# Thresholded attention and a maxout feed-forward on one core: scores negated into z by the maximum pass, the threshold in an instruction of its own, and a new order of issue

## The chip, the core and the metric

The kernel runs on one core of a Trainium2 chip. Its engines are named as in the profile: PE (TensorE, matmuls; PEld is its weight load), DVE (VectorE), ACT (ScalarE), POOL (GpSimd) and SP (SyncE, which here only issues DMAs). The metric is the device time of one execution in microseconds. For a change of this kernel, about 1% is what a measurement can tell from none.

## What is computed

Attention over 8 batches and 8 heads, 576 positions, head width 64, in fp32. In each row of scores, those more than tau (0.02) below the row's maximum are dropped before the softmax. Then a feed-forward layer takes the maximum of three products elementwise and multiplies it by an output matrix.

```python
scale = 1.0 / np.sqrt(q.shape[-1])
scores = scale * np.matmul(q, k.transpose(0, 1, 3, 2))
thresh = np.max(scores, axis=-1, keepdims=True) - tau
scores = np.where(scores >= thresh, scores, -1000000000.0)
scores = scores - np.max(scores, axis=-1, keepdims=True)
attn = np.exp(scores)
attn = attn / (np.sum(attn, axis=-1, keepdims=True) + 1e-09)
attn_out = np.matmul(attn, v)
# x: attn_out as 4608 rows of 512
h = np.maximum(np.maximum(x @ w1, x @ w2), x @ w3)   # 512 to 768
out = h @ w_out
```

## The kernel before

**Tiling.** Four heads of one batch are a quad; there are 16 quads. A quad has nine chunks, each of 128 rows of queries and keys of all pairs that belong together, and each chunk two halves (r = 0 and 1) of 128 rows by 576 scores. So there are 144 chunks and 288 halves; a half is the unit of the softmax.

**The way of a half.** Each step is a letter in the order (below). S: PE writes the scores of a half into one of four PSUM slots of two banks each (line 280, `scores`). m: DVE takes the row maximum out of PSUM (line 307, `maximum`). e: ACT makes the first pass, reads the same PSUM slot and writes z, an fp32 tile in SBUF for both halves of a chunk (line 318, `exponents`). Then the second pass makes the masked numerators in place in z and sums them (line 326, `numerators`). r: DVE takes the reciprocals of the chunk's two sums. p: POOL multiplies z by them and writes P in bf16, one instruction for each half. t: SP issues a DMA that transposes P into the quad's tile ptq. O: PE multiplies ptq by v.

**Two ways for the two passes.** The string MASKED has a digit for every half. For "1", ACT's first pass is an exponential of score minus maximum, and DVE drops what is below exp(-tau) and sums, in one instruction (letter k). For "0", ACT's first pass is a leaky rectifier of the distance below the threshold, with the slope FLAT = 2**-100 on the kept side, and ACT's second pass is an exponential with scale -1/FLAT that brings the kept ones back to their size and the dropped ones to zero, and sums (letter n). Of the 288 digits 97 are ones.

**Maximum.** For masked halves it is a reduction with the sign turned (`nm` is minus the maximum). For the others it is a pass that subtracts tau, keeps the maximum in an accumulator (`nm` is the maximum minus tau, which the rectifier takes as its bias), and writes a bf16 result that nobody reads (`unused`).

**The rest.** T: PE transposes q or k; ACT (a) and DVE (c) take them out of PSUM, POOL swaps the halves of q (q). F and B: PE's feed-forward pieces, first and second part; h (ACT) and v (DVE) take the hidden pieces out, u (ACT) the output rows, o stores them. x and w take the products out. l loads q, k and v, y casts v, g loads a piece of weights, z casts it on POOL.

**The order.** The string ORDER holds one letter for each step, with a digit for the PSUM slot behind S, T, O and F. The program walks through it and issues one step at a time, and `_Ordered` (line 80) keeps each engine's instructions in that order. Nothing is rearranged: an instruction that waits holds up all that stands behind it on its engine. There are four PSUM slots (SLOTS), four z tiles (ZBUFS), six P tiles (PBUFS). In the kernel before, the first quad's loads, transposes and swaps are issued ahead of the order.

The lines that say what is chained to what in the two passes:

```python
scalar.activation(out=zn, in_=sc, func=AF.Exp, bias=bias)                              # masked, first pass
scalar.activation(out=zn, in_=sc, func=AF.Prelu, bias=bias, scale=-1.0, alpha=FLAT)    # not masked, first pass
vector.scalar_tensor_tensor(out=zn, in0=zn, scalar=thr, in1=zn,
                            op0=OP.is_ge, op1=OP.mult, accum_out=acc)                  # masked, second pass
scalar.activation(out=zn, in_=zn, func=AF.Exp, scale=-1.0 / FLAT, accum_out=acc)       # not masked, second pass
```

Of the kernel before, what the change touches and what calls it, by code (L numbers as in the profile page):

```python
# [23 lines left out]
MASKED = """
101001010001010101001000101000011001001100001100001001000010001000001000
000100111100100100010010100000011000100001110011101000000100000001001001
000100010110111000011000100000001101000011110101010000000011000001000001
011001111000110001000010001100000010010000101010100110001000011100010010
"""


# [5 lines left out]
ORDER = """
lllS0lmyeS1lylS2ymllS3kelmnlS0mleS1rlepmlT2kpnlS3elrmpalS0mtepS2meyT1mntS3cqekqnlT1S0mellyarkT2ynlS1mplermlp
eS3lcepS0tmnS2qmS1eqlrmnpS3lkeptnmS0pemlekytS2emT1nrT3mlpnlrcpelkpT3etS0raS2mpnlS1mqetkapS0emS3gnpmS2eryrtkp
eT1mnS0qlcelmpS1nlS3mpntmpermeptS2kepS0nmlS1yertkperS3mnplO2melprmtepS0wnS1qmetS2pmnS3pelrkztnO0memeplS1rknl  # L40
qT2lewmgpakS3gnpS2tmepxrrmS1epT0tmeS3pnkS2ptnmezrmeS1keqgT3cnS2pamS0npmtS3eprmeS1pmteS2pmeS0myteT3knO1znlrcl
emS3plnrO2lpmngwpekpxS1teS0rwmF2npS3mteqBrmepS1khF0qteF2mnBpS3evqBnmF1pS0nrvztBemS2phS3rgempF1nmF0ptBekzBevS
2nS3rvpnF1gmpF0ntBmzeBekS2pghF3rmnS1ptveBzmF0nS2vpeBgrmT3ptS1hazmT0eS3cqegF2mpT0BkatF1nzvS0eBrrmpnS2gvS3pemO
1qntrmeznF0wpT2geBrcpnS1S3pthmS2npmO0eytmqekpS1eF3wrxmS2qBepmF0nF1yvtpeBS3znvBlnrF2pmlhS0lrpBetmF1pnS3vzeBtm
S2npvS0nlpmF1elmetkS3eS2rnrmplS0BlmpelmpetS3kepF2mnlkutT0eBkarrokpuS3luS0rmouS1pmoO2epmetqeT3pwS0nocT1pS2atm
qO3nmqepT1xwS0qcteS3mnF1mS2eBkeF0mhF3nrBkpS1evBnpmF2nS0vtBermS3phS1epmF2nmF0tBerkpBerS3vnF1prmS2nptBveyrmF0h
S3kepT1BmaS2pvteF1pmnF0BkpteS3vBnqS2mhS1pmeF0rtmepS3BreymqF2nvT1yBeplcS0nlyS3vtnT1mO2yapmelprelS1wpS0tnmO3qn
mpleklS2eF1wtrxmpT0nBcqS3lekpF0lhmS2lnBrtmpeS1vepS3lmnF0ytF2meBkeBlrS1vphlS3mnlpF0mS2letBrmepF1rnvpS3leBptmS
0nyvF2emlT1puS3lnkF2tarmpeS1kopeS0mBnlqmetrS3kepS1urmF0lupomeyokS2pntT3meBpcelS1rkuptS3umT2O0ymeoqknoO1arkle
qwlS2xplwT3rnmF0lpS1tceyBmF3hplS2eBlqmF0ntpS1vepBmnlF3rS2tvepBnmpF0hlS1teBmF3nvS2elBmF0lnS1rvepBmpS3hS2emtF0  # L50
mF1eBkeBrnrF3vpF2nyvS0pnBmptS1hrBpmeS3ptveT0maT2S1cnqS0empS2nrmO3ptemqeF1pweS0kntBT3mnO2rvepakF1xqT0wnS3cyBn
plrmS2hlyS0metF1qmeBplS3evS2plnrF0mlpnF1tmyBeykBpeS3lvnF2lmS0htBrepmF1nprlS3veBlpmS2ntpvF0eyrmS1tunS3kpF0emo
nprmS2elpBrmtepekS1ptuS3mF2upmeonS0tkS1ermBpnompelS3kleO0tmuurkpeT1owS2aoS3ymnlT0qO1mleplceqtT2xwkS0aT3rF1mn
lqS2lcepBlmF3qhlS0kpeBlmF1nS2vteBmnF3rS0revpBnmpF2hS1kpteBmF3pvS0eBtmnF2S1veBrkpS3hF0mF2pmeBrBtepvF1npS3vnBy
tmS0hF2keT1lmBalS3rrvpelS1mlnpF2lS0mpetBrmeqO3vpelnptS1wnT2pF0mnS3ytceBmS2hS1repmS0nqmO3epmeryktF2yxT1ewBkpS
3avF0nqmT1nqlcS2BeplmF1nlS3vetBrrmpF0hS2kpleBmlF1nlpS3vetBpmnF0vntS2rurS1pemS0yoF3mempelS2kpleS1tmnBpmeklS0e
tS2rumpF1umpeokT3oeT0rtBkankqS2cluT3qumoS0aprS1oemS3pnkO2ptemnO0pmerqrtweqS1wxS2pmnF3pmS0eyBtpmeF1hkpT2BeclS
3nvlF0tnS2rmpF1meBplBevtS3nF2mS0hlBemF1nrS3rvpeBmpF2nS0vpetBmpF1hkS3teBmF2nS0veBmnF1rF3vepBknpS2hT0BmaS1trve
pS0mnpS3meO2trrempnT1qwS0epcF2nT3pmtS1aqBemF3qvS0epBrknpS2thmO1nqmepS3wxrF0ptemT1pBceS2tvnS1F3mnF0meBrBepvF2
nyS1kplhBrmlF3ylvS0eBtnmpS2vF1pelmT3luS0nrktpF1emakoS2nqS3rmeBlpmleqtrS0ekpS2umF3ulpmnokS1peoBtermpkeS0lyuS2  # L60
tmuS1pnmO3ypeomoekO0tewnkS2lxS1rwnpmF3lmT0peBlcetS2khF0T1rrmS3plaBlnmF1qlevplBpS2etvF0qnmT3pnlcS1BetmS3hrS2r
pmeS0lpmF1elkpleBtmF3nS2pveBmntF1S0veBrrnmpF3hS2kpBemF1npS0vtnBprmS3epvteS2mynF1mS0eyByepmlS3hlF2metF1rkBepT
0nvBlS3palrvS2nlyS0mtnO1mpempleO3kqntweT2qwxrS1cnpT0S3mapF2meT0qtBrcepS1rhT0qmF3aS2keBqmF0nS1pvnBpmteS3vyepS
2mnF0tmS1eBrrempT3hcpS2nF0ptmeF3ykBepT1vnBS2qatvF0nqmS1qurreT3pomnpcS0F2ekptnS3mnS1pmBemterS0epS3mupF1urompe
tkS2npS0meBonktermS3purO2kyuomeoS1nwpS0nmpO2emperkO3ytxO1werykpS2xtxF0mS3pBemptF1hpS2eBmtnF0S3veBmnF1vnS2Bem
S0hrO3mpeF1kpeS2xBnmF0tS3veBmnF1rS2vepBmpF0hS3rkpteBmF1npvF2eBrktnpS0BvF3pmhS1kteO2rmpBxF0epvS2nBtmF1S3rvepB
mpF0hS2etBmF1F3veBknF0vBF2hS1nBBvO3vF0mO2uoF0xneS2BmrwpF1upeoS3ntBmurkeopF2F0hF3pnvF2vtF0rhF3puvF2rpvF0ohF3p
tvF2vpF0hF3vtF2vF0hF3vF2vF0hF3uvF2voO1uoO0wF3xF2F1hF0vF2vF1hF0vF2vF1hF0vF2vF1hF0vF2vF1hF0vF2vF1hF0vBvF2uuooB
F1uuouoo
"""  # L70


# [28 lines left out]
def kernel(  # L101
# [437 lines left out]
    warm = bank("warm", 3)  # L539
    for _ in range(WARM):  # L540
        tensor.transpose(warm[:, 0:128], identf, identf)
    for _ in load(0, first=True):
        pass
    for x, (r, n) in enumerate(((0, "q"), (0, "k"), (1, "q"), (1, "k"))):
        p = transposed(Ls[0], n, r)
        p.first(x)
        p.done[0]()
        if n == "q":
            for _ in swapped(Ls[0], r):
                pass  # L550
# [146 lines left out]
```

## Time and profile before

| what | value |
|---|---|
| runs of the kernel | 473.0, 475.19 and 476.6 us, median 475.19 |
| the profiled execution, first to last instruction (span) | 470.4 us |
| what lies between that span and the runs | 2.6 to 6.2 us, 4.8 to the median |
| mean granted TensorE clock | 0.977 of full speed |

The profiled execution's time outside its span is not listed apart, so sums are made against the span and then set beside the runs' median. In the profile each engine's share of busy time is an average over the whole span, and the stages of this kernel differ, so the tables by windows say more. A row such as "ACT ACTIVATE z<-sc,nm ... x288 | 207.6, 742 | 27.5 <-DVE nm" reads: ACT wrote z from sc (scores in PSUM) and nm 288 times, 207.6 us in all, 742 ns each, and was idle 27.5 us just before such instructions, which a maximum of DVE ended most often. Neighbouring instructions of one engine overlap: the time from one start to the next, in the timeline, is what an instruction takes from the engine, and it is less than its length.

### The profile page before, as it was taken

What the parts mean: (1) busy time and instruction counts of PE and PEld (TensorE: products, weight loads), DVE (VectorE), ACT (ScalarE), POOL (GpSimd) and SP (SyncE); (2) the same over time, 40 slices, a digit from 0 to 9 for tenths busy, and PEclk for the clock granted to TensorE, in tenths of its full rate; (3) what the DMA queues carried; (4) which work ended last, traced back from release to release, by engine and by line L of the source; (5) the groups of instructions that cost most, each with busy time, mean ns of one, the idle gap of its engine ahead of it and who ended that gap; (6) DMA issues with size and microseconds to landing.
All of it is one profiled execution on the core that took longest, in us unless ns stands there. A gap on an engine that the chain in (4) does not pass through costs nothing.

```text
span 470.4 us, 13953 instructions
## 1 busy us (share of the span) xinstructions
PE 438.7 (93%) x5188; PEld 311.7 (66%) x5188; DVE 396.3 (84%) x994; ACT 398.7 (85%) x818; POOL 318.6 (68%) x416
## 2 busy tenths in 40 slices
PE   7865777999999999989999999999999999999995
PEld 5443534767577767857677676878676776778862
DVE  4998595988989999879899998998899999795541
ACT  4989496989999998998998999899999999875622
POOL 3888585989768876667865887558857888560500
PEclk8979798999999999999999999999999999999999
DMA  7999999999997999998999999987899899572712
GB/s 219 262 223 202 232 187 258 225 244 212 167 262 118 145 223 204 232 224 155 208 228 198 177 229 188 193 152 142 164 252 222 177 122 215 103 119 47 169 35 102
DMA packets 213285, 87.44 MB, mean 186 GB/s; under 512 B 186336, under 2 KB 200160, under 8 KB 213216
## 3 DMA queue, kind: packets, MB, share of 16 engines
q1 hardware_dynamic: 212656, 85.95, 88.2%
q8 instruction: 41, 0.67, 0.6%
q10 hardware_dynamic: 560, 0.59, 0.4%
q14 instruction: 28, 0.23, 0.1%
HBM read 34.60 MB, written 9.44 MB: 94 GB/s over the span
## 4 chain that ended last, share of the span: by engine, by line
PE 67%; ACT 10%; DVE 10%; DMA 5%; issue 5%; POOL 2%; POOLq 0%; ACTq 0%; DVEq 0%
PE ph L89 24%; PE sc L89 24%; PE po L89 9%; ACT z L89 8%; PE o L89 7%; DMA ptq<-P 4%; DVE unused L89 3%; DVE z L89 3%; PE tp L89 2%; POOL P L89 2%; DVE nm L89 2%; DVE kt L89 1%; DMA qm<-in_q_dram 1%; ACT hm L89 1%; ACT qt L89 1%
## 5 line engine op out<-in xcount | busy, mean ns | idle before, releaser
L89 POOL TENSOR_SCALAR P<-z,rs 128x576 bf16<-128x576 f32 x288 | 232.0, 818 | 104.6 <-DVE rs L89 61.6
L89 ACT ACTIVATE z<-sc,nm 128x576 f32<-128x576 f32 x288 | 207.6, 742 | 27.5 <-DVE nm L89 10.3
L89 PE MATMUL sc<-kt,qt 64*128 64x320 f32 (+2 forms) x640 | 193.5, 437 | 3.8 <-ACT z L89 2.8
L89 PE MATMUL sc<-kt,qs 64*128 64x256 f32 (+2 forms) x640 | 190.5, 427 | 6.0 <-ACT z L89 4.0
L89 PE MATMUL ph<-xt,w 64*128 64x288 bf16 (+2 forms) x2160 | 175.0, 283 | 1.0 <-DVE kt L89 0.3
L89 DVE TENSOR_SCALAR_CACHE_REDUCE unused<-sc 128x576 bf16<-128x576 f32 x191 | 141.4, 749 | 20.3 <-PE sc L89 19.4
L89 PEld LDWEIGHTS <-w 64*128 64x128 bf16 (+1 forms) x2160 | 126.8, 94 | 38.9 <-issue 10.6
L89 ACT ACTIVATE z<-z 128x576 f32<-128x576 f32 x191 | 129.9, 684 | 0.3
L89 PEld LDWEIGHTS sc<-kt,qs 64*128 64x128 f32 (+1 forms) x640 | 91.3, 181 | 29.0 <-ACT z L89 13.9
L89 PEld LDWEIGHTS sc<-kt,qt 64*128 64x128 f32 (+1 forms) x640 | 91.4, 181 | 19.7 <-ACT z L89 11.0
L89 DVE SCALAR_TENSOR_TENSOR z<-z 128x576 f32<-128x576 f32 x97 | 84.3, 870 | 1.1 <-ACT z L89 0.6
L89 DVE TENSOR_REDUCE nm<-sc 128x1 f32<-128x576 f32 x97 | 71.9, 750 | 9.0 <-PE sc L89 8.4
L89 POOL COPY qs<-qt 64x640 f32<-64x640 f32 (+1 forms) x62 | 44.8, 722 | 15.6 <-ACT qt L89 12.2
L89 PE MATMUL po<-wo,hT 64*128 64x512 bf16 (+1 forms) x480 | 54.3, 357 | 0.1
L89 PE MATMUL o<-ptq,vb 128*64 128x512 bf16 (+2 forms) x544 | 42.2, 290 | 9.7 <-DMA ptq<-P 9.1
L89 DVE TENSOR_TENSOR hm<-ph,hm 128x576 bf16<-128x576 f32 (+2 forms) x54 | 37.0, 685 | 11.8 <-PE ph L89 11.2
L89 ACT ACTIVATE hm<-ph 128x576 bf16<-128x576 f32 (+2 forms) x54 | 32.1, 595 | 17.1 <-PE ph L89 16.9
L89 PEld LDWEIGHTS <-vb 128*64 128x64 bf16 x544 | 24.2, 113 | 27.1 <-issue 16.5
L89 PEld LDWEIGHTS <-hT 64*128 64x128 bf16 (+1 forms) x480 | 28.5, 97 | 20.1 <-issue 6.6
L89 DVE TENSOR_TENSOR hT<-ph,hm 128x576 bf16<-128x576 f32 (+2 forms) x54 | 36.9, 684 | 2.8 <-PE ph L89 1.2
L89 ACT ACTIVATION_READ_ACCUMULATOR z<-z 128x1 f32 x191 | 38.5, 202 | 0.0
L89 DVE CAST xt<-o 128x576 bf16<-128x576 f32 (+2 forms) x30 | 14.4, 486 | 13.0 <-PE o L89 10.7
(30 smaller groups left out, 257.1 us busy)
## 6 DMA issues: line engine op xcount, KB each, us to landing
vm<-in_v_dram SPq DMA_DIRECT2D x64, 128.0 KB, 3.2
out_dram<-ob SPq DMA_DIRECT2D x32, 256.0 KB, 2.9
qm<-in_q_dram SPq DMA_DIRECT2D x15, 512.0 KB, 4.5
km<-in_k_dram SPq DMA_DIRECT2D x15, 512.0 KB, 5.3
stage<-in_moe_w_dram SPq DMA_DIRECT2D x9, 512.0 KB, 4.7
ptq<-P SPq DMA_TRANSPOSE x144, 3.9
stage<-in_moe_w_out_dram SPq DMA_DIRECT2D x3, 512.0 KB, 4.2
qm<-in_q_dram SPq DMA_DIRECT2D x16, 64.0 KB, 2.5
```

The costliest lines, as they stand in the source:

```text
L89: ins = fn(*a, **kw)
```

## The change

There are four parts.

1. DVE's maximum is one form for all halves. It multiplies the scores by -1, writes them in fp32 into z, and keeps their minimum in the accumulator, so that `nm` is minus the maximum. z is taken there, not at the first pass. The reduction and the `unused` tile go.
2. For halves that aren't masked a DVE instruction on one column (letter s) makes the threshold `th` = maximum - tau from `nm`.
3. ACT's first pass reads and writes z in place: the exponential with scale -1, the rectifier with bias `th`. It reads PSUM no more.
4. ORDER and MASKED are made anew. 72 halves are masked (25 fewer). The first quad's loads, transposes and swaps now stand in the order too, and the feed-forward's `hm` tile is kept for each f.

```diff
@@ load
         if first:
             for n, src, e in srcs:
                 e.dma_start(out=L[n][:, 0:8], in_=rows_of(src)[:, 0, 0:8])
+                yield
@@ maximum, exponents
-    def maximum(g, idx, r, sc):
-        nm = small.tile([128, 1], F32, name="nm")
-        if masked(g, idx, r):
-            vector.tensor_reduce(out=nm, in_=sc, axis=AX, op=OP.max, negate=True)
+    def maximum(c, r):
+        if r == 0:
+            c["z"] = zz.tile([128, W], F32, name="z")
+        nm = c["nm", r] = small.tile([128, 1], F32, name="nm")
+        vector.tensor_scalar(out=c["z"][:, r * S:(r + 1) * S], in0=c[r], scalar1=-1.0, scalar2=None,
+                             op0=OP.mult, op1=OP.min, accum_out=nm)
+    def threshold(c, r):
+        th = c["th", r] = small.tile([128, 1], F32, name="th")
+        vector.tensor_scalar(out=th, in0=c["nm", r], scalar1=-1.0, scalar2=tau, op0=OP.mult, op1=OP.subtract)
+    def exponents(c, r):
+        zn = c["z"][:, r * S:(r + 1) * S]
+        if masked(c["g"], c["idx"], r):
+            scalar.activation(out=zn, in_=zn, func=AF.Exp, bias=c["nm", r], scale=-1.0)
         else:
-            unused = small.tile([128, S], BF16, name="unused", bufs=2)
-            vector.tensor_scalar(out=unused, in0=sc, scalar1=tau, scalar2=None,
-                                 op0=OP.subtract, op1=OP.max, accum_out=nm)
-        return nm
-    def exponents(g, idx, r, z, sc, bias):
-        zn = z[:, r * S:(r + 1) * S]
-        if masked(g, idx, r):
-            scalar.activation(out=zn, in_=sc, func=AF.Exp, bias=bias)
-        else:
-            scalar.activation(out=zn, in_=sc, func=AF.Prelu, bias=bias, scale=-1.0, alpha=FLAT)
+            scalar.activation(out=zn, in_=zn, func=AF.Prelu, bias=c["th", r], alpha=FLAT)
@@ ffn
-                    st["hm"] = hp_.tile([128, nr, n], BF16, name="hm", bufs=3)
-                hm = st["hm"]
+                    st["hm", f] = hp_.tile([128, nr, n], BF16, name="hm", bufs=3)
+                hm = st["hm", f]
@@ ahead of the order
-    for _ in load(0, first=True):
-        pass
-    for x, (r, n) in enumerate(((0, "q"), (0, "k"), (1, "q"), (1, "k"))):
...
@@ flows and issue
-                T=((g, n, r) for g in range(1, NQ) for r in range(2) for n in "qk"),
+                T=((g, n, r) for g in range(NQ) for r in range(2) for n in "qk"),
...
-                 l=(None for g in range(1, NQ) for _ in load(g)))
+                 l=(None for g in range(NQ) for _ in load(g, first=g == 0)))
...
             c, r = line["m"].pop(0)
-            c["bias", r] = maximum(c["g"], c["idx"], r, c[r])
+            maximum(c, r)
             line["e"].append((c, r))
+            if not masked(c["g"], c["idx"], r):
+                line["s"].append((c, r))
+        elif what == "s":
+            threshold(*line["s"].pop(0))
         elif what == "e":
             c, r = line["e"].pop(0)
-            if r == 0:
-                c["z"] = zz.tile([128, W], F32, name="z")
-            exponents(c["g"], c["idx"], r, c["z"], c[r], c["bias", r])
+            exponents(c, r)
```

The new order begins so (before: `lllS0lmyeS1lylS2ymllS3kelmnlS0mleS1r`, behind the first quad's loads):

```
llllllglT0T1laclT2laT1lclgzlqqS2llqqS1mS0semS2nsS1mleyS3mlS0nsmyS2lesS1rmlpelmS3nyplmnS0te
```

More of the change, by code (lines that the diff above doesn't have):

```diff
@@ L24 @@
 MASKED = """
[L25 to L28, printed above, removed]
+000011000000001100000000000101010000010010000001010001000100000100000100
+000100010100010001000000100000010011010000100001011100000000100000010100
+010001001011000000010000110000100100000010110000011010000000001000001000
+000001110001100011000100000000100100010000011001100010000110000001001010
 """
@@ L37 @@
 ORDER = """
[L38 to L67, printed above, removed]
@@ L68 @@
-tvF2vpF0hF3vtF2vF0hF3vF2vF0hF3uvF2voO1uoO0wF3xF2F1hF0vF2vF1hF0vF2vF1hF0vF2vF1hF0vF2vF1hF0vF2vF1hF0vBvF2uuooB
-F1uuouoo
+llllllglT0T1laclT2laT1lclgzlqqS2llqqS1mS0semS2nsS1mleyS3mlS0nsmyS2lesS1rmlpelmS3nyplmnS0teS2rmpssT1emplekzT3
+leklalrsmeS1lmpnT0lsnspS2stnyrmacS1pelsmeplS3egqnT2tqT0ecnsmS2tnrpS1ermpnS3ptmnpmT2eqmetqrsskepS3egskaS1pnT0
+nrmptemS3ysepscS1eqtmnS2rqsmnplS3nsmpT1eS2stmemnS3snrS2lrspelpelymeplnS3sclpnlrS1mznlmS2pelmS3pgnrstyemO1akp
+etmrpseS2tS3pemS0npmT2etkS3nssrkpaterT2wepmT1nlqmS0ntqsseprS3meyyS0nmpspS3teceqmS2npmlS0nktO3rssrepmempT2npt
@@ new lines @@
+S0swcnpmS2eztS0emzsmnS2gseS0srmpgekS2lpaxslS1reS3ptmnpO0snmqtermpnS2smnO1pleqlmetS3rwpS2ewmS0pxlnszF1mlnF3sm
+qBgekF2thF0keBsBervpBnrS1pvhS3ptmeF2epmS0BnmtF3nsvS1eBsrsmpF2eS0knpBvnF1rhtrpBmeS2pvT0nS3lspmaS1tmzeT2F0sesk
+zF3leBmBlvpS1lhrcS0nplmS3nplT2mF1eqlmF0agynBsrssgT3evpS2leclpF1nmBtqS3evqBnktO0ersrepmS2thpswS3epS1mnF0lpmnS
+2qsmBnS3zrsemS1epgO2svepmnzF0mnF3wregkS1pBxtssmBeprS2veS1tpmhF0npmS3nBytmyS1nysvF2eT3tsrmBpaT0vnpT1S3tcayS2z
+essS1rmetzT0meS3cpeS2klnpF0lnrslnpmBlepmterF1spukuptnS3BermpelmpS0ulkS2qulS3nsmS1lesmqlO0ertsqmeO2pmnpwleS3t
@@ new lines @@
+sqsxwkS0nF2nmF1tBerrmpBhS3pevS2ptF0smeF1pmnS3tBnssmBerF2vphoT3skBeplS1avlS0emF3tnF2mBnrpS0lnvBplemT1S3thrssc
+pS0eF2smynpT1lBmntS3vaS0ermpS2elmF1pnF3lssqmnBlT0syelvF2eBlcyBthkS0nrvS3peF1mpF2eBqtmnBnrsvS0pS3hrsspmF1eS2p
+tmeS0pmeS3nqBmoF2nqmlF0erlBssvpeF3lkpBetBvhF1nvS0tnS2rmpBnmS3peT0vteF2rmpS1uskepT3F2esmaktS1ncBerskpemS3nS0r
+pmnS1putmO3uyrssmeqlS0ewpS1lnpmS3noS2pmelS0ssrsmeplO1eklpnmO3tesymnO2rwonwplxpS0wrxtS1pmeS2pemS3tT0qsmeF1yem
+tnkS2T3akBnqslmelycF0eqF2lkuBluBsrkhptF3erT1vBapF2vnpS1teS0pmS3nmyBtF1srhsmpS0eS2opsmeS3ymeBoF0mnF2lrnvBptBn
@@ new lines @@
+vpS1hssS3rtmepT2T0empS1ascqtS3nmT0qnF2mqF1leBcqelBrvpS0lssS3evlpF2lnymF1lnBrsskpleO0mlhnrlpS3welS2pmS0etpmBn
+yS3mnF2lsrsemF0poBevplBesF3vtnS1kBhrmF2eptT0veBpnS1vtS3asrmF2peF0spmnlS1BtnkyBmhF3qevS2tS1nrsmpS0emBpeF2sste
+kO1umernvS2pS0nmpF3xtmnsT2esrrS0pceoBpmnoyketpS2uS0wmuS1pnrlsmS3lepmS2oS0pnsmF1erompeS3lmpeT2lsBqnmlakteT0qk
+O2uketsreO3rscqewplS0xwS2plumS3nlpmF1ntpS0mnS2ssrmS3epoBmnpF0thF2ymeBssrByetvyF3pnsS1vpnS0tmBerS2mphF1slmepS
+3elF0keF2lmBlnsBtvnBrnS3vpS1htrspmS0epmS2etF3pnsmF1nBmBelrvpT2leF0katF3kBeqBsvhF2leyvT0lT1cBalpS3nsrvS1ptemS
@@ new lines @@
+0pnS2mqS3tsemO1qnmqlnmO0yoerswpeT3wspS1xcS2ntmF3emF0eBsskF2hBknT3rrBvpaS1repvF3eS0ptmS2npmBnS1pmthS0pssmeT2F
+3ctnF1reBsmpT2snBvpS0arqtvS3eS2mpeS1mpeS0mnqtF3snkqF2emluqrnsS1mlpT3elBclpelemO0lursskpuoeO1klnlrwS2xpowS3nm
+pS1ertmS0pnS2smpS3estF1pmemnS0mtnBresmpktyF3uT0surBpaS1lphS2lmeS0pmlS3eF1mteF2meBknBtF3snvF0essrBvpBhkyF2nF3
+veBrS0epvS1nptsmBnS2pmF0eslsS1rmhplBempT2tesS3vynS1ysmqteF0cqF3eBrmnpoBvnT1poS2shrS0lpmaS3lempS1leF2symlT0eB
+mtynO3vnskntF1weF2rrBcnpBvnpS0shsS3ptmeS1pmS2eqF0mtnF3qmnBrBsserpsvF2epS1veS0ptmBepF3mnS1kthF0snsmBBnrvpS1eT
@@ new lines @@
+2vpF3asrytmepS0S1upmnT2qS3mtnS0ceqS1rmnlS2psosmO3eplnmlS0xrswpS1metF3pesemtT2eBkamnlqO0serlkpulkO1uoewopS2xw
+rS0npmlS1npmlS3eF2lrsmpelmpeT0lF1secqlBnsktnkS0urBrpmutS3hpS2meS1plmeS0pF3tmeyF2sesBmF1elkT0nlBvBatvF3hT0skn
+S2tcBnF1rermpF0oeBvpBlnvpS3ohS2pmeoS0qnmlF1S3lsmqeT2tsBmyeyF0rnkpF3taBrssveBpeS2vptS1nmpS0hmS2norF3ssmpetF1m
+eyBBnsvpF2nS0vtnS3rmBpeS1shprmF0nptS2meS3psmBeqmF1lnF2svteBkBS0srhvpS3emT2peO1cqtemnF0kT3nlrsBwpalS2rvpeS1sm
+S3qetF0mnqF2mnplT1usT3nycBpaS2rvpteS1mS3eqS0sespmF2nqtsmeT1kBnslrecpoS3rmupS1uS0pmlnS2pmnoS3erO1smpempeO0tse
@@ L70 @@
+mnkO2etkxwS3rwxpS1tnwpmS0eS2srmeF3ptnkpeF1rmBnptmpkBuS2ythF0smuS1yesrBmeS2pvnS1pS3ssemtO0nmF2xsmeF1oskeF3oBe
+rpBoveF0phBtnBvF1nrS2vpnS3mpnS0mBetF2mhS3BmF1rvF0pBkpBS2svhS3eytmF0emF1BsssekF3eBrvpBevS0yhpS2nF3tmnF1rsmF0p
+nBeprBsvnBptnS3vpS2hrmtpS1emS0peS3mntF2smeF1sBmeS0veBmnO2sO3kxF0vxnO2sO1xeF3wekuerkoF2pnrnBrprptBupuptF0upF3
+hF1pvtF0vpF3hF1vF0tvF3hF1vF0voF3hF1ovF0voF3hF1vF0vF3hF1vO0vF3xuO1uoO2woF3xF2F1hF0vF2vF1hF0vF2vF1hF0vF2vF1hF0
+vF2vF1hF0vF2vF1hF0vBvF0uuoBoF3uuouoo
 """
@@ L541 @@
         tensor.transpose(warm[:, 0:128], identf, identf)
-    for _ in load(0, first=True):
-        pass
-    for x, (r, n) in enumerate(((0, "q"), (0, "k"), (1, "q"), (1, "k"))):
[L545 to L550, printed above, removed]
     def chunks():
@@ L581 @@
     todo = dict(S=((c, r) for c in chunks() for r in range(2)),
-                T=((g, n, r) for g in range(1, NQ) for r in range(2) for n in "qk"),
+                T=((g, n, r) for g in range(NQ) for r in range(2) for n in "qk"),
                 O=products(), F=pieces())
-    line = {k: [] for k in "menkrptahvuxwcq"}
+    line = {k: [] for k in "menkrptahvuxwcqs"}
     casts = iter([w[1] for w in wl])
```

## The prediction

> **What bounds the kernel now.** I read the page's first part, then busy time by stages.
>
> ```profile
> span 470.4 us, 13953 instructions
> PE 438.7 (93%) x5188; PEld 311.7 (66%) x5188; DVE 396.3 (84%) x994; ACT 398.7 (85%) x818; POOL 318.6 (68%) x416
> ```
> ```profile
> core 0: us, PE busy (x) PEld busy (x) DVE busy (x) ACT busy (x) POOL busy (x), PEclk, DMA share, GB/s
> 0.00:90.00 90.00, 67.28 (x594) 43.48 (x596) 70.19 (x184) 70.53 (x143) 65.33 (x86) 0.89 0.99 222
> 90.00:420.00 330.00, 326.46 (x4093) 236.25 (x4092) 303.49 (x759) 306.72 (x630) 244.34 (x320) 1.00 0.94 190
> 420.00:470.40 50.40, 44.95 (x508) 31.96 (x502) 22.60 (x53) 21.44 (x47) 8.88 (x12) 0.99 0.38 95
> ```
>
> There are three stages. Up to 90 us the softmax runs almost alone; ACT is idle for 19.5 us of it. From 90 to 420 us softmax and feed-forward are mixed: PE shows 326.5 of 330 us, ACT 306.7 (idle 23.3), DVE 303.5 (idle 26.5). The last 50 us are PE's: ACT and DVE work less than half of them. PE's 99% in the middle is no proof that PE alone sets the pace, since its ends are modelled; three engines are each within 8% of full, and every half chunk passes through all of them in turn. Next, the groups and the waits.
>
> ```profile
> L89 ACT ACTIVATE z<-sc,nm 128x576 f32<-128x576 f32 x288 | 207.6, 742 | 27.5 <-DVE nm L89 10.3
> ...
> L89 DVE TENSOR_SCALAR_CACHE_REDUCE unused<-sc 128x576 bf16<-128x576 f32 x191 | 141.4, 749 | 20.3 <-PE sc L89 19.4
> ...
> L89 ACT ACTIVATE z<-z 128x576 f32<-128x576 f32 x191 | 129.9, 684 | 0.3
> ...
> L89 DVE SCALAR_TENSOR_TENSOR z<-z 128x576 f32<-128x576 f32 x97 | 84.3, 870 | 1.1 <-ACT z L89 0.6
> ```
> ```profile
> PEld sc L89 <- ACT z L89: 24.9, 53, 1.7
> ...
> PE sc L89 <- ACT z L89: 6.9, 13, 1.2
> ...
> ACT z L89 <- POOL P L89: 3.2, 8, 1.0
> ```
>
> The reader sees a ring: PE's weight loads and matmuls of new scores wait for ACT's first pass, which still reads the PSUM slot; ACT sits idle 27.5 us before that pass, most of all for a maximum of DVE (nm). The waits of PE for ACT are what the change goes at. The chain of waits adds two holes of another kind, with the stretch around the first by windows:
>
> ```profile
> 44.02 4.98 DMA ptq<-P
> ...
> 68.88 5.05 DMA ptq<-P
> ```
> ```profile
> 48.00:54.00 6.00, 4.87 (x33) 3.68 (x35) 1.63 (x3) 0.06 (x2) 1.96 (x3) 0.57 1.09 248
> ```
>
> A product (O) stands in PE's queue ahead of new scores and waits about 5 us for the last transposing DMA. ACT works 0.06 us in the 6 us around it.
>
> **The change part by part.** *ACT, first pass (exponents).* It now reads z in SBUF instead of PSUM, still with a bias vector. No such form is in the trace, so I bound it by starts in ACT's timeline.
>
> ```profile
> 24.34 0.73 ACT L89 ACTIVATE z<-sc,nm 128x576 f32<-128x576 f32 x1
> 24.96 0.68 ACT L89 ACTIVATE z<-z 128x576 f32<-128x576 f32 x1
> 25.54 0.19 ACT L89 ACTIVATION_READ_ACCUMULATOR z<-z 128x1 f32 x1
> 25.63 1.36 ACT L89 ACTIVATE z<-sc,nm 128x576 f32<-128x576 f32 x2
> ```
> ```profile
> 359.12 0.64 ACT L89 ACTIVATE hm<-ph 128x576 bf16<-128x576 f32 x1
> 359.65 0.74 ACT L89 ACTIVATE z<-sc,nm 128x576 f32<-128x576 f32 x1
> ```
>
> From start to start: PSUM with bias vector 0.62 us, PSUM without one (hm) 0.53, SBUF without one (z<-z) 0.58. So the vector costs 0.09 and SBUF 0.05; both together 0.67. Against 0.62 to 0.64 now I take +0.04 us, times 288 = +11.5 us. The ends are 0.58 (the vector is free from SBUF: -0.05 x 288 = -14 us) and 0.74 (no overlap at all: +0.11 x 288 = +32 us). The value taken lies nearest the z<-z row, the only one that reads SBUF.
>
> [...]
>
> *ACT, second pass.* MASKED has 72 ones instead of 97: 25 numerators go from DVE to ACT, at 0.58 + 0.09 us (24.96 to 25.63) = 0.67 each, +16.8 us. ACT in all: +28 us, 398.7 to 427. By place, counted in the two masks: of the first 64 halves 22 and 14 are masked, of the next 192 63 and 48, of the last 32 12 and 10. So the first stage gets 64 x 0.04 + 8 x 0.67 = 8 us, the middle 192 x 0.04 + 15 x 0.67 = 18 us, the end 2.6 us.
>
> *DVE.* These rows price its parts.
>
> ```profile
> 25.38 0.75 DVE L89 TENSOR_REDUCE nm<-sc 128x1 f32<-128x576 f32 x1
> 26.05 0.74 DVE L89 TENSOR_SCALAR_CACHE_REDUCE unused<-sc 128x576 bf16<-128x576 f32 x1
> 26.72 0.08 DVE L89 DVE_READ_ACCUMULATOR unused<-sc 128x1 f32 x1
> ```
> ```profile
> 28.98 0.15 DVE L89 RECIPROCAL rs<-sm 128x2 f32<-128x2 f32 x1
> 29.05 0.73 DVE L89 TENSOR_SCALAR_CACHE_REDUCE unused<-sc 128x576 bf16<-128x576 f32 x1
> ```
> ```profile
> L89 DVE COPY kt<-tp 128x640 f32<-128x640 f32 x16 | 13.1, 818 | 0.1
> ```
>
> Reduction and maximum pass both take 0.67 us from start to start, and the accumulator's read, 0.08 us long, starts as the maximum's 0.67 us are over, so all 288 maxima in the one form cost 0 to 97 x 0.08 = 8 us more (I take 3). Writing fp32 is free: the kt copy, PSUM to SBUF in fp32, has 64 more columns and takes 69 ns more. The threshold is a one-column instruction; the nearest row, the reciprocal, holds the engine 0.07 us (28.98 to 29.05) and at most its 0.15: 216 of them are +15 us, at most +33. Twenty-five numerators less are 25 x 0.87 = -22 us. Sum -4 us, between -7 and +19; DVE stays near 393 and below ACT. That it must wait for its own maximum's result happens rarely: in the order 16 of 216 thresholds stand right behind their maximum.
>
> *PE and PSUM.* A score's slot is now free after the maximum, not after ACT. In the order the distance from S to the last reader of the slot falls from 14 letters (S to e, median) to 9 (S to m), while e stands 24 letters behind m instead of 7. So the waits for ACT above (24.9 and 6.9 us) go, and ACT always has work in front of it. What is late next is ACT itself. PE's work is the same.
>
> *A new wait.* z is taken at the maximum, so DVE waits for POOL's pass over the chunk four earlier. Behind a waiting maximum stand thresholds, numerators, reciprocals, kt copies and the feed-forward maxima; PE waits for the slots, POOL for the reciprocals.
>
> *The order.* The first loads go through it. POOL's first weight cast (z) now stands ahead of the first swap, and its load (g) ahead of the v loads.
>
> ```profile
> 6.37 0.95 POOL L89 COPY qs<-qt 64x640 f32<-64x640 f32 x1 [5.06 <-ACT qt L89]
> ```
> ```profile
> 2.22 3.35 SPq L89 DMA_DIRECT2D vm<-in_v_dram  x4
> ```
> ```profile
> stage<-in_moe_w_dram SPq DMA_DIRECT2D x9, 512.0 KB, 4.7
> ```
> ```profile
> L89 POOL CAST w<-stage 128x1024 bf16<-128x1024 f32 x9 | 10.4, 1153 | 3.0 <-DMA stage<-in_moe_w_dram 3.0
> ```
>
> The weight load takes the place of the first v load on SP: issued near 2.2, landed 4.7 later at 6.9, cast until 8.1, swap until 9.0, against 7.3 now: the first score comes 1.5 us later (0 to 3). It lies on the path, since ACT has nothing before it. In exchange the ninth transposing DMA stands 54 and 47 letters ahead of the product in the first two groups, against 31 and 24, so the two holes should close: 0 to 10 us of idle ACT, of which I take 8. The last part is unchanged: behind the 33rd score from the end stand 65 F, 25 B and 11 O instead of 67, 27 and 10. The transposes' DMAs come later behind their P (10 letters, before 7) on SP's queue; I cost that at nothing, since products wait for them less. If POOL or SP is late, six P buffers fill and POOL stalls. The split of hm by f changes no instruction.
>
> *Sum, against the 470.4 us span.* Start +1.5. First stage: 8 us more on ACT and 8 us of holes closed: 0. Middle: 306.7 + 18 = 324.5 us of ACT work; the stretch where ACT is fullest today shows what the queue can reach:
>
> ```profile
> 360.00:390.00 30.00, 29.87 (x402) 22.09 (x400) 28.70 (x71) 29.62 (x65) 26.56 (x37) 1.00 0.93 174
> ```
>
> At 29.62 of 30 it would take 329 us (-1); at twice that idle time, 2.5%, 333 us. I take 332, +2. End 0, with ACT far below full. Together +3.5: a span of 474. The three runs' median, 475.2, is 4.8 above the span, so about 478 us, 0.6% above the median: no change that a measurement here can tell (about 1%).
>
> **The rivals.** *Slower: the z tiles bind.* The middle has 226 half passes of POOL:
>
> ```profile
> 90.00:420.00 330.00, 64.36 (x150) 257.34 (x523) 181.50 (x226) 1.00 0.94 190
> ```
>
> That is a chunk each 2.92 us, so four z tiles allow 11.7 us from first use to POOL's end. By the order's text this life grows from 61 letters of 19.3 per chunk (3.2 chunks) to 70 of 21 (3.3 chunks). Once real delays add 0.7 chunk, 2 us, DVE waits, and with it all that stands behind a maximum. For it: ACT already waits 3.2 us for POOL with the shorter life. Against it: those waits are 8 in 288. Price: ACT keeps today's 7% idle in the middle: 324.5 / 0.929 = 349 us, +19; with the start +21, about 496. Half that, +11, gives 486; from about +5 it counts as slower.
>
> *Faster: ACT's pass isn't dearer.* If the bias vector is hidden from SBUF, or 0.62 stays, the middle gets 10 us, not 18: 317 us, 321 at 1.3% idle, -9; the first stage gains 8 - 5 = 3, the start loses 1.5. About -11: 464. For it: PE's 32 us of waits for ACT go. Against it: the two differences of the ACT rows.
>
> *The slots are hidden anyway:* PE still waits as now, because the maxima are late; ACT then idles as in the slower rival, at most the same 496.
>
> **How the numbers follow.** No change 0.37, at 478 us (470 to 480 by the 1% bound). Slower, by z tiles, late maxima or ACT's dearer end: 0.35. Faster, by a cheap pass or by more closed holes: 0.28. The range of 8 in 10 reaches from 463 (the faster rival) to 492, between half and full price of the slower one; cases of both signs hold most of it, so the likeliest one's own range is 472 to 483.
>
> **What would show it.** The first pass over z: 0.67 us from start to start, about 0.76 long, right; 0.62 or less, the faster rival. ACT busy near 425, DVE near 393, in the middle ACT's idle share under 3%. PE's waits for ACT's z gone from the table of waits. DVE waiting for POOL's P: under 3 us right, over 10 the slower rival. The transposing DMA gone from the chain near 44 and 69 us. Wrong would be an ACT that is idle 7% as today, or a DVE above 410.

## The result, and the profile after

The changed kernel takes 459.98 us (median of 4 runs, 458.28 to 460.99) against 474.12 us for the kernel before on the same chip (473.0 to 476.6). The ratio is 0.968 with a 95% interval of 0.964 to 0.972: 3.2% faster. The prediction was 478 us, 0.6% more than before, with a range of 463 to 492. It was wrong: the kernel became faster, and its time lies 3 us below the range.

The profiled execution has a span of 457.4 us, 13.0 less than before. It took 459.19 us, 1.8 more than its span, and the kernel's other executions are 1.8 us longer than theirs too. By the same 1.8 us the profiled execution of the kernel before took about 472 us (an estimate), some 2 us less than its median. So the two spans lie closer together than the medians, and most of the 4.8 us that the prediction added to its span were not time outside the span. These are its busy times, then the three stages, with the columns of the prediction's second fence.

```profile
span 457.4 us, 14215 instructions
...
PE 435.7 (95%) x5188; PEld 318.1 (70%) x5188; DVE 392.0 (86%) x1257; ACT 414.5 (91%) x868; POOL 303.8 (66%) x416
```
```profile
0.00:90.00 90.00, 75.25 (x684) 49.80 (x686) 73.81 (x247) 80.37 (x166) 66.39 (x93) 0.91 1.01 229
90.00:420.00 330.00, 328.03 (x4189) 246.72 (x4186) 304.59 (x978) 320.43 (x672) 231.22 (x316) 1.00 0.99 191
420.00:457.40 37.40, 32.43 (x324) 21.53 (x320) 13.65 (x34) 13.75 (x32) 6.15 (x8) 0.99 0.41 100
```

ACT worked 70.5 us of the first 90 before and now works 80.4. Between 90 and 420 us it is idle for 9.6 us where it was idle for 23.3. The last stage is 13 us shorter because the span ends earlier: less work is left at 420 us (PE is busy for 32.4 us behind it instead of 45.0).

The groups, by line, operation and tile (busy us, mean ns of one, idle before):

```profile
L91 DVE TENSOR_SCALAR_CACHE_REDUCE z<-sc 128x576 f32<-128x576 f32 x288 | 209.6, 751 | 13.7 <-PE sc L91 5.6
...
L91 ACT ACTIVATE z<-z,th 128x576 f32<-128x576 f32 x216 | 159.5, 768 | 6.9 <-DVE th L91 6.5
...
L91 ACT ACTIVATE z<-z,nm 128x576 f32<-128x576 f32 x72 | 54.0, 768 | 0.0
```

The maximum that writes z is as long as the old one (751 against 749 ns). ACT's first pass became longer, 768 against 742 ns, but the idle time before it fell from 27.5 us to 6.9. The table of waits of the changed kernel (us in total, times, longest):

```profile
PEld sc L91 <- DVE z L91: 20.3, 43, 2.3
...
ACT z L91 <- DVE th L91: 6.5, 14, 2.0
...
PE sc L91 <- DVE z L91: 5.4, 10, 1.7
...
DVE z L91 <- POOL P L91: 5.0, 14, 1.1
...
PE o L91 <- DMA ptq<-P: 0.3, 1, 0.3
```

PE's 31.8 us of waits of scores for ACT's z are down to 1.1, but 25.7 us of waits for DVE's maxima stand in their place. What vanished with nothing in its place is the last row. Before, it read:

```profile
PE o L89 <- DMA ptq<-P: 9.1, 3, 4.8
```

### The profile page after: what moved, and what is told of

Its sections match the earlier page's. It is cut to its first block, busy times and chain, and to the rows that moved or that the text cites. A ratio compares the mean times of both kernels' runs of the same rounds, so it can differ in the third digit from the quotient of the medians.

```text
span 457.4 us, 14215 instructions
## 1 busy us (share of the span) xinstructions
PE 435.7 (95%) x5188; PEld 318.1 (70%) x5188; DVE 392.0 (86%) x1257; ACT 414.5 (91%) x868; POOL 303.8 (66%) x416
## 4 chain that ended last, share of the span: by engine, by line
PE 62%; ACT 19%; DVE 10%; issue 4%; DMA 2%; POOL 1%; SPq 0%; ACTq 0%; DVEq 0%; POOLq 0%
PE ph L91 25%; PE sc L91 22%; ACT z L91 16%; PE po L91 8%; DVE z L91 7%; PE o L91 6%; PE tp L91 2%; DMA qm<-in_q_dram 1%; DMA ptq<-P 1%; POOL P L91 1%; ACT ob L91 1%; DVE hm L91 1%; ACT qt L91 1%; ACT hm L91 1%; DVE kt L91 1%
## 5 line engine op out<-in xcount | busy, mean ns | idle before, releaser
L91 POOL TENSOR_SCALAR P<-z,rs 128x576 bf16<-128x576 f32 x288 | 221.5, 783 | 104.8 <-DVE rs L91 47.8
L91 DVE TENSOR_SCALAR_CACHE_REDUCE z<-sc 128x576 f32<-128x576 f32 x288 | 209.6, 751 | 13.7 <-PE sc L91 5.6
L91 PE MATMUL sc<-kt,qt 64*128 64x320 f32 (+2 forms) x640 | 185.2, 441 | 2.5 <-DVE z L91 1.5
L91 ACT ACTIVATE z<-z,th 128x576 f32<-128x576 f32 x216 | 159.5, 768 | 6.9 <-DVE th L91 6.5
L91 PE MATMUL ph<-xt,w 64*128 64x288 bf16 (+2 forms) x2160 | 163.4, 283 | 0.8 <-ACT xt L91 0.3
L91 ACT ACTIVATE z<-z 128x576 f32<-128x576 f32 x216 | 145.1, 675 | 0.5
L91 DVE SCALAR_TENSOR_TENSOR z<-z 128x576 f32<-128x576 f32 x72 | 60.1, 845 | 1.1 <-ACT z L91 1.0
L91 ACT ACTIVATE z<-z,nm 128x576 f32<-128x576 f32 x72 | 54.0, 768 | 0.0
L91 DVE TENSOR_TENSOR hm<-ph,hm 128x576 bf16<-128x576 f32 (+2 forms) x54 | 37.0, 685 | 13.5 <-PE ph L91 11.8
L91 PE MATMUL o<-ptq,vb 128*64 128x64 bf16 (+2 forms) x544 | 39.6, 282 | 0.8 <-issue 0.5
L91 PEld LDWEIGHTS <-hT 64*128 64x128 bf16 (+1 forms) x480 | 26.9, 97 | 18.0 <-issue 2.1
L91 DVE COPY kt<-tp 128x640 f32<-128x640 f32 (+1 forms) x31 | 23.3, 750 | 6.7 <-PE tp L91 6.6
```

The source lines that it names most:

```text
L91: ins = fn(*a, **kw)
```

## Where the 13 us lie

To compare like with like, each trace was cut where the same maximum starts: the 1st, the 32nd, the 64th and the 256th of 288. The rows are windows (length, then busy time of PE, PEld, DVE, ACT and POOL, then clock, DMA share, GB/s). The kernel before:

```profile
0.00:8.60 8.60, 5.46 (x53) 4.34 (x54) 2.81 (x10) 3.07 (x4) 2.63 (x9) 1.00 0.70 212
8.60:45.00 36.40, 28.04 (x213) 16.95 (x213) 34.63 (x91) 33.31 (x68) 30.00 (x39) 0.86 0.98 229
45.00:98.00 53.00, 41.77 (x433) 27.46 (x435) 39.62 (x103) 41.58 (x88) 39.87 (x48) 0.90 1.08 226
98.00:380.10 282.10, 278.67 (x3501) 202.58 (x3501) 260.08 (x651) 262.52 (x537) 208.27 (x276) 1.00 0.97 195
380.10:470.40 90.30, 84.75 (x998) 60.37 (x994) 59.13 (x146) 58.21 (x125) 37.79 (x47) 1.00 0.54 113
```

The changed kernel:

```profile
0.00:9.70 9.70, 6.86 (x54) 5.96 (x56) 2.41 (x10) 3.13 (x4) 1.38 (x7) 1.00 0.79 238
9.70:49.30 39.60, 32.47 (x236) 20.50 (x233) 33.46 (x112) 37.32 (x80) 31.90 (x44) 0.78 0.97 236
49.30:92.80 43.50, 38.39 (x425) 24.52 (x424) 40.73 (x134) 42.28 (x90) 34.94 (x46) 1.00 1.07 217
92.80:368.90 276.10, 274.66 (x3506) 208.41 (x3504) 256.64 (x828) 271.13 (x566) 201.40 (x275) 1.00 1.04 202
368.90:457.40 88.50, 83.33 (x982) 58.65 (x976) 58.79 (x177) 60.68 (x132) 34.15 (x48) 0.99 0.60 119
```

The start is 1.1 us longer and the first 31 halves 3.2 longer. The next 32 halves, which hold the two holes that the prediction quoted from the chain, are 9.5 us shorter (53.0 to 43.5), although ACT does 0.7 us more work in them: its idle time there falls from 11.4 to 1.2 us. The middle is 6.0 us shorter although ACT does 8.6 us more. The end is 1.8 us shorter.

Each kernel has one trace, and the start differs between executions. The same code up to the first maximum took 8.6 us here and 9.3 in before_dma_less below; with the changed start it took 9.7 here and 8.3 to 10.7 in the experiments. So the 1.1 us of the start are about the size of that spread.

## The experiments

Two theories stood after the result. *Slots:* PE waited for ACT to let go of the PSUM slots, and the new passes end that. *Holes:* the time came from the products that no longer wait for the transposing DMA. As for what sets the pace now, ACT at 91% was the first suspect; the rivals were DVE, PE, the DMAs, or several of them together. Each kernel was timed beside the kernel before on its chip. The medians of the kernel before lie between 474.1 and 475.9 us on these chips, so the ratios compare better than the times, and a difference of 2 us between two times is not told from none.

### The parts of the change

**The new passes in the order of before** (passes_old_order), with the mask of before, a threshold one DVE step behind its maximum, and 24 of POOL's passes a few letters earlier:

```diff
-llllllglT0T1laclT2laT1lclgzlqqS2llqqS1mS0semS2nsS1mleyS3mlS0nsmyS2le
+llllllllllllT0aqqT1cT2aqqT3clllS0lmyeS1lylS2ymllS3kselmnlS0mleS1rsle
```

> The three new passes (maximum into z, threshold, first pass in place) with the order and the mask of before: thresholds put in one DVE step behind their maximum, 24 of POOL's P passes moved a few letters earlier so that four z tiles suffice. Theory Ring (the PSUM slot that is free earlier brings the gain): 458 to 466 us. Theory Order (the gain needs the new order: lead of e over m, holes closed): 474 to 484 us, since ACT gets 288 x 0.04 = 11 us and DVE 191 thresholds more and nothing stands earlier.

**The same, with the first pass reading PSUM again** (passes_psum), so that the slot is held until ACT, while the maximum still writes z:

```diff
-            scalar.activation(out=zn, in_=zn, func=AF.Exp, bias=c["nm", r], scale=-1.0)
+            scalar.activation(out=zn, in_=c[r], func=AF.Exp, bias=c["nm", r])
...
-            scalar.activation(out=zn, in_=zn, func=AF.Prelu, bias=c["th", r], alpha=FLAT)
+            scalar.activation(out=zn, in_=c[r], func=AF.Prelu, bias=c["th", r], scale=-1.0, alpha=FLAT)
```

> As passes_old_order, but ACT's first pass reads the scores in PSUM as before (DVE writes z for nothing), so that the slot is held until ACT is done. Theory Ring: 12 us or more above passes_old_order. Theory Order: within 3 us of it, or faster by up to 10, since the pass from PSUM is 0.04 us cheaper.

**The changed kernel with the lead taken out** (no_lead): each first pass is moved up in the order, to three letters behind its threshold or maximum, so that it stands 8 letters behind the maximum (median) instead of 24. The thresholds move up with them, to 6 letters behind the maximum instead of 12:

```diff
-llllllglT0T1laclT2laT1lclgzlqqS2llqqS1mS0semS2nsS1mleyS3mlS0nsmyS2le
+llllllglT0T1laclT2laT1lclgzlqqS2llqqS1mS0semS2nsS1melyS3mslS0enmsyS2
```

> The changed kernel with each first pass (e) moved up in the order to three letters behind its threshold or maximum, the threshold one DVE step behind its maximum: e stands 8 letters behind m instead of 24. Theory Ring: 458 to 463 us, the slot does not depend on e. Theory Order: 467 to 478 us, because ACT waits for DVE again at each pass.

| kernel | us | ratio to before (95%) |
|---|---|---|
| changed | 459.98 | 0.968 (0.964 to 0.972) |
| passes_old_order | 507.79 | 1.070 (1.065 to 1.075) |
| passes_psum | 518.90 | 1.094 (1.087 to 1.100) |
| no_lead | 518.01 | 1.090 (1.084 to 1.097) |

The passes without the order lose 7%, and no_lead loses 9%, both far more than either theory expected; passes_psum lies 11.1 us above passes_old_order, close to the 12 of the theory Ring. The waits of passes_old_order, then of passes_psum, then of no_lead:

```profile
ACT z L91 <- DVE th L91: 52.1, 70, 2.4
...
DVE z L91 <- POOL P L91: 33.5, 48, 1.8
...
PEld sc L91 <- DVE z L91: 6.6, 16, 1.0
```
```profile
PEld sc L91 <- ACT z L91: 56.8, 98, 1.7
ACT z L91 <- DVE th L91: 55.9, 74, 2.5
...
PE sc L91 <- ACT z L91: 22.0, 40, 1.3
```
```profile
ACT z L91 <- DVE th L91: 49.1, 63, 2.0
DVE rs L91 <- ACT z L91: 39.2, 47, 2.4
```

In the old order ACT stands 52.1 us before thresholds, and DVE 33.5 us before POOL's P: that is the wait of the prediction's slower rival, the z tiles, in full size. In no_lead it is again ACT's wait for thresholds, 49.1 us, and behind it DVE's for ACT. So the distance of threshold and first pass from the maximum carries the changed kernel: taking it out costs 58 us. The pair passes_old_order and passes_psum prices the freed slot by itself: holding it brings 78.8 us of PE waiting back and costs 11 us net of what the first pass saves by reading PSUM. The slots theory is right in that much, but these two kernels stand in an order in which other waits are long, so the 11 us are not a share of the 14 that the change gained. The new order with the old passes was not tried: counted in the order, 284 of the 288 slots that scores fill would be taken again ahead of the first pass that must free them.

### What sets the pace now

**Relief of one engine or path at a time**, all in the changed kernel:

```diff
@@ no_bias
-            scalar.activation(out=zn, in_=zn, func=AF.Exp, bias=c["nm", r], scale=-1.0)
+            scalar.activation(out=zn, in_=zn, func=AF.Exp, scale=-1.0)
...
@@ no_threshold (no letter s in the order either)
-            scalar.activation(out=zn, in_=zn, func=AF.Prelu, bias=c["th", r], alpha=FLAT)
+            scalar.activation(out=zn, in_=zn, func=AF.Prelu, bias=c["nm", r], alpha=FLAT)
@@ pe_less
-                    my["h"] = halves([[operands(kc, a) for kc in range(4)] for a in range(2)])
+                    my["h"] = halves([[operands(kc, a) for kc in range(3)] for a in range(2)])
@@ dma_less (five of the nine 128-column blocks of P; the products read block m for both halves)
-        sync.dma_start_transpose(out=L["pt"][:, :, c["idx"] * 128:(c["idx"] + 1) * 128], in_=c["P"])
+        sync.dma_start_transpose(out=L["pt"][:, 0:5, c["idx"] * 128:(c["idx"] + 1) * 128], in_=c["P"][:, 0:640])
```

> The changed kernel with ACT's first pass without a bias vector (the maximum and the threshold are left out of the exponents; the thresholds are still made): 0.58 us instead of 0.67 from start to start, 288 x 0.09 = 26 us less for ACT. Theory ACT (ACT sets the pace of the changed kernel, 2% idle in its middle): 440 to 450 us. Theory PE (PE's queue sets it): 456 to 460 us.

> The changed kernel without the threshold instructions (the rectifier takes minus the maximum for its bias, so the cut is at another place): DVE -216 x 0.065 = 14 us, and ACT's 6.5 us of waits for thresholds go. Theory ACT: 454 to 460 us, at most the waits. Theory DVE (DVE sets the pace): 444 to 450.

> The changed kernel with a quarter of the split hidden products left out (three of four steps over the model width in seven batches): 504 matmuls of 288 columns less, some 34 us of PE at peak pace, all else in place. Theory PE (PE's queue sets the pace of the changed kernel): 425 to 435 us. Theory ACT (ACT, 2% idle in the middle, sets it): 450 to 458 us. Theory All (PE, ACT and DVE are level, relief of one gives nothing): 452 to 460.

> The changed kernel with four of the nine blocks of each transposing DMA left out (the products read the first five blocks for both halves of the pairs, so PE's work is the same): the DMA stream and SP's issue shrink by about 100 us of 374. Theory DMA (the stream of DMAs through SP, 27 of 30 us busy, sets the pace of the changed kernel): 435 to 450 us. Theory All (PE, ACT, DVE and the DMA stream are level): 455 to 459.

**Work moved between ACT and DVE**: MASKED with 25 digits fewer (mask_47), 12 more (mask_84) and 25 more (mask_97) than the 72, the letters n, k and s of the order following. The first row of mask_97:

```diff
-000011000000001100000000000101010000010010000001010001000100000100000100
+000111000000011100000001000101010010010010010001010001100100000110000100
```

> The changed kernel with 25 more numerators moved from DVE to ACT (47 masked instead of 72), letters otherwise in place: ACT +25 x 0.67 = 17 us, DVE -20. Theory ACT: 472 to 478 us. Theory PE: 459 to 464 us.

> The changed kernel with 12 numerators moved back to DVE (84 masked): ACT -8 us, DVE +9.5 less 12 thresholds of 0.065. Theory ACT: 453 to 457 us. Theory PE: 459 to 461. If DVE is as near the limit as ACT: 460 to 465.

> The changed kernel with as many masked halves as before (97): ACT -17 us (to about 398), DVE +18 (to about 410). Theory ACT: 446 to 452 us. Theory PE: 459 to 461. If DVE then binds: 463 to 470.

**Several reliefs together**: no bias vector and no threshold (act_dve_less); these and pe_less (all_less); these three and dma_less (dma_all_less).

> The changed kernel with both reliefs at once: the first pass without a bias vector and no thresholds (the maximum and the threshold are left out of the exponents), ACT -26 us and DVE -14 us. Theory PE: 455 to 460 us. Theory All, with ACT and DVE the nearer two: 445 to 453.

> pe_less and act_dve_less together. Theory PE: as pe_less. Theory All: 425 to 440 us, well below each of the two, since nothing is left at its limit.

> all_less (452.4 us: three of four steps of the hidden products, no bias vector, no thresholds) with the shorter transposing DMAs as well. Theory DMA: 415 to 435 us. If what is left is the order's own waits or the z tiles: 445 to 452.

| kernel | us | ratio to before (95%) | against the changed kernel's 459.98 |
|---|---|---|---|
| no_bias | 459.12 | 0.965 (0.958 to 0.972) | -0.9 |
| no_threshold | 457.85 | 0.964 (0.959 to 0.969) | -2.1 |
| pe_less | 458.85 | 0.968 (0.963 to 0.972) | -1.1 |
| dma_less | 459.63 | 0.969 (0.963 to 0.974) | -0.4 |
| mask_47 | 471.88 | 0.992 (0.989 to 0.996) | +11.9 |
| mask_84 | 464.40 | 0.978 (0.973 to 0.983) | +4.4 |
| mask_97 | 471.55 | 0.994 (0.991 to 0.997) | +11.6 |
| act_dve_less | 458.81 | 0.966 (0.961 to 0.972) | -1.2 |
| all_less | 452.42 | 0.955 (0.950 to 0.959) | -7.6 |
| dma_all_less | 443.77 | 0.935 (0.930 to 0.940) | -16.2 |

The busy times of no_bias, then of mask_47, then of mask_97:

```profile
PE 430.9 (94%) x5188; PEld 317.8 (69%) x5188; DVE 389.2 (85%) x1257; ACT 392.3 (86%) x868; POOL 306.6 (67%) x416
```
```profile
PE 438.3 (93%) x5188; PEld 317.1 (67%) x5188; DVE 376.1 (80%) x1232; ACT 430.1 (91%) x918; POOL 298.1 (63%) x416
```
```profile
PE 440.2 (94%) x5188; PEld 316.5 (67%) x5188; DVE 408.5 (87%) x1282; ACT 401.8 (85%) x818; POOL 313.9 (67%) x416
```

No_bias takes 22 us of work from ACT and gains nothing that can be told from zero, so ACT alone does not set the pace, though it is the fullest engine but PE. Cut at the same maxima, its middle is even longer than the changed kernel's, 279.2 us against 276.1, with ACT busy for 257.5 of them; POOL now waits 5.9 us for the transposing DMAs before it may write P, against 0.3. The interval of each single relief overlaps that of the changed kernel. In pe_less PE's busy time fell by 15 us, not by the 34 expected, which is 504 times the 0.068 us of such a matmul where 40 of them run in a row (2.72 us, from 203.48 in the changed kernel's timeline). Yet 16 us more on ACT (mask_47) or on DVE (mask_97) cost 12 us each, although the other engine gets relief. The waits say where, for mask_47 and then for mask_97:

```profile
DVE rs L91 <- ACT z L91: 26.2, 36, 2.5
```
```profile
ACT z L91 <- DVE th L91: 22.6, 25, 2.0
```

Their middles, from 90 to 420 us, in the same order:

```profile
90.00:420.00 330.00, 320.34 (x4040) 237.32 (x4038) 284.49 (x931) 322.50 (x688) 223.70 (x310) 1.00 0.95 189
```
```profile
90.00:420.00 330.00, 321.61 (x4054) 237.72 (x4052) 310.13 (x974) 301.52 (x611) 237.47 (x313) 1.00 0.97 190
```

In mask_47 ACT is full (322.5 of 330 us). In mask_97 it is otherwise: DVE works 310.1 us and ACT 301.5, and neither is full. The order was made for the 72 masked halves and got no new arrangement for 97, so the order's own waits are a rival to a full DVE there, and no run separates the two.

The changed kernel is near level: no single engine or path sets its pace. Three reliefs together bring 7.6 us, and the DMA cut, worth 0.4 us alone, brings 8.7 more on top of them (452.42 to 443.77; the intervals of the ratios do not meet). But a kernel in which nothing but the full engines counts should have gained more: 425 to 440 us were expected of all_less, and 415 to 435 of dma_all_less if the DMAs are what is left. What holds the last one at 443.8 us, with ACT busy for 88% of its span and DVE for 85%, was not found; the waits within the order and the z tiles are left as suspects. In all_less the z tiles show again as the next wait, 17.6 us where the changed kernel has 5.0:

```profile
DVE z L89 <- POOL P L89: 17.6, 32, 1.5
```

### What the holes were worth

The holes theory says that the kernel before, with shorter transposing DMAs and nothing else changed, gains most of what the change gained, while the changed kernel (dma_less above) gains nothing from the same cut. The edit of before_dma_less in the kernel before is that of dma_less.

> The kernel before with the same four of nine blocks of each transposing DMA left out. Theory Ring (before, the waits between PE, ACT and DVE set the pace; only the two holes of 5 us go): 464 to 470 us. Theory DMA (the stream set the pace before too): 445 to 460.

It took 460.66 us, ratio 0.971 (0.965 to 0.977): 13.5 us less than the 474.17 of the kernel before on that chip, and as fast as the changed kernel. That is just above the range of the theory DMA and well below that of the theory Ring. Its wait of products for the DMA, and its windows by the same maxima:

```profile
PE o L89 <- DMA ptq<-P: 0.3, 1, 0.3
```
```profile
0.00:9.30 9.30, 6.72 (x54) 5.74 (x56) 2.40 (x9) 3.07 (x4) 2.80 (x9) 1.00 0.68 202
9.30:45.30 36.00, 26.88 (x220) 14.92 (x219) 34.68 (x92) 33.34 (x68) 30.11 (x39) 0.95 0.95 229
45.30:88.80 43.50, 38.77 (x428) 26.46 (x425) 39.98 (x101) 41.19 (x88) 40.25 (x49) 0.96 0.97 201
88.80:368.30 279.50, 277.62 (x3499) 202.21 (x3501) 258.94 (x649) 262.30 (x536) 208.28 (x275) 1.00 0.73 152
368.30:458.30 90.00, 84.54 (x999) 60.37 (x994) 59.21 (x146) 58.31 (x125) 37.88 (x47) 1.00 0.35 81
```

The 32nd to 63rd halves take 43.5 us, as in the changed kernel. Of the 12.1 us of span that the cut saves, 9.5 lie there and 2.6 in the middle; the other stretches differ by less than 1 us each. Set against this kernel, the changed one is 0.4 us longer in the start, 3.6 longer in the first 63 halves, 3.4 shorter in the middle and 1.5 shorter at the end: together 0.9 shorter. So the holes are the size of the whole gain, and all the rest of the change, which adds 16 us of ACT work and frees the slots early, comes out even. What made the first 63 halves longer was not tried. The granted clock is a suspect: in the rows from the first maximum to the 32nd it is 0.78 in the changed kernel and 0.95 here, and PE is busy for 32.5 us against 26.9.

That two kernels are equal does not by itself show that they saved the same time. The windows do show it for the 9.5 us. For the 2.6 us of the middle, where the third product wait of the kernel before lies or where shorter DMAs may help otherwise, it stays open. A kernel before whose holes are closed by its order, with whole DMAs, was not tried.

## Why the prediction was wrong, step by step

Two steps of its sum failed. In the middle it let ACT's work alone set the pace ("What is late next is ACT itself"): 18 us more of it, at today's smallest idle share, gave +2. The middle came at -6.0. ACT's work grew by 8.6 us there, and no_bias shows that the pace does not follow ACT's work. In the first stage it set 8 us of closed holes against 8 us of added ACT work and had 0. The stage came at -6.3, and the stretch with the two holes alone gained 9.5.

**The prices of single instructions held.** ACT's and DVE's timelines of the changed kernel (start, length; a row with x2 holds two):

```profile
200.83 1.43 ACT L91 ACTIVATE z<-z,th 128x576 f32<-128x576 f32 x2
202.16 0.67 ACT L91 ACTIVATE z<-z 128x576 f32<-128x576 f32 x1
```
```profile
203.25 0.75 DVE L91 TENSOR_SCALAR_CACHE_REDUCE z<-sc 128x576 f32<-128x576 f32 x1
...
203.92 0.15 DVE L91 TENSOR_SCALAR th<-nm 128x1 f32<-128x1 f32 x1
203.99 0.15 DVE L91 RECIPROCAL rs<-sm 128x2 f32<-128x2 f32 x1
```

Two first passes take 202.16 - 200.83 = 1.33 us, 0.67 each, as predicted, and one is 768 ns long, against a predicted 0.76 us; a threshold takes 0.07 (203.92 to 203.99); the maximum that writes fp32 takes 0.67 (203.25 to 203.92), and the accumulator's read, 0.08 us long, hides: it starts at 203.92 together with the threshold. DVE's 392.0 us stand against a predicted 393.

**The holes were sized as idle time of ACT in the holes themselves: 8 us, of 0 to 10.** They were worth 9.5 us there and about 12 in all. The prediction read both holes as about 5 us, the length of the DMAs in the chain; PE's own waits there are 4.8 and 2.9 us, and the third wait, at 210 us, is 1.3. It also saw the row with clock 0.57 behind the first hole and did not price it. The windows of the kernel before, cut at the end of the wait, show why a wait of 4.8 us costs more than it lasts:

```profile
44.30:49.10 4.80, 0.05 (x1) 0.00 (x0) 1.45 (x6) 3.52 (x9) 4.64 (x8) 0.71 1.11 250
49.10:52.60 3.50, 3.46 (x23) 2.33 (x25) 0.76 (x1) 0.00 (x0) 0.86 (x1) 0.50 1.00 224
```

When the products may start, at 49.1 us, TensorE runs for 3.5 us at half its clock (0.50), and they stand ahead of the next scores; ACT does nothing for those 3.5 us.

**ACT's added work was mis-sized: 28 us predicted, 15.9 measured (398.7 to 414.5).** This is the most mis-sized term of the sum. In the middle it was 18 us against 8.6 (262.5 to 271.1). The added price was taken between back-to-back starts (0.67 against 0.62 to 0.64), but it was added to a busy time in which many instructions stood alone. Worked out from the starts of all ACT instructions, 62 of the 288 first passes before were followed by a pause and counted with their whole 0.742 us; the mean was 0.66. Now 30 stand alone and the mean is 0.68. So the first passes added 5 us, not 11.5. The second passes, with their reads, added 13 instead of 16.8, since 42 of their reads stood alone before and 12 do now. ACT's other instructions fell by 2.

**The idle share held.** The prediction took 1.3 to 2.5% idle for ACT in the middle; it is 5.0 of 276.1 us, 1.8%, where it was 7%. With the measured 271.1 us of work instead of 18 us more, its own sum would have given 275 to 278 us for this stretch, and 276.1 came. But no_bias shows that this sum is only a description: with 22 us less on ACT the time stayed. ACT is late next, as predicted, but not alone: relief of any one engine gained nothing. Of the middle's 6.0 us, shorter DMAs bring 2.6 in the kernel before; which part of the change brings the other 3.4 was not separated.

**The first stage was put at 0 and came at -6.3 us**: -9.9 from the holes (by before_dma_less) instead of -8, and +3.6 from the rest instead of +8. ACT's added work there was 4.7 us; whether it, the clock or the order cost the 3.6 is open. **The start** cost 1.1 us, predicted 1.5 (its own ends, 9.0 against 7.3 us, give 1.7), and the agreement is luck. The weight cast did come first on POOL, at 9.0 us instead of 6.9, but the first score began at 8.2 us, before POOL's swap, which began at 10.1. So it was 0.5 us later than before (7.7), and not by the path described. The rest is PE: the first score's first matmul was 0.79 us long against 0.45 before, although the windows list a clock of 1.00 for both starts. **The end** was put at 0 and came at -1.8; nothing was tried on it.

**The waits.** PE's waits of scores for ACT's z are all but gone, as predicted, but PE waits 25.7 us for the maxima instead of nothing, which is what the third rival said of PE; its other half, an idle ACT, did not come. DVE's wait for POOL's P is 5.0 us, between the 3 that would have been right and the 10 of the slower rival; that rival came in full where the order was left as it was. The faster rival's time, 464 us, was nearest, but its reason, a first pass no dearer than before, is false; more closed holes, named beside it as a second way to be faster, was the way it went.

Taken together: by the measured stretches the sum is +1.1 - 6.3 - 6.0 - 1.8 = -13.0 us, where the prediction had +1.5 + 0 + 2 + 0 = +3.5. Half of the gap is the middle (8.0), and most of the other half the first stage (6.3).

## What to carry to other kernels

Price a wait at the head of an in-order queue by the window until the engines behind it are full again, not by the wait: here 9.1 us of product waits were worth about 12, if the whole gain of before_dma_less is put down to them. When a price from back-to-back starts is added to a busy time, take the base from starts too, since busy time counts the tail of each instruction that stands alone (a first pass was 0.74 us long here and took 0.62 to 0.64 from start to start), and a change that closes gaps takes those tails away (62 first passes stood alone before, 30 do now). Here four resources were each near full: relief of one gained nothing, and 16 us more work on one cost 12. Judge such a change by its order and its slack, and test reliefs together.
